# Decode attention beside an MLP on one core: `wo` is loaded and multiplied ahead of the first 16 rows of `w4`, and those rows go as four segments of 256 columns

## The chip, the core and the metric

The kernel runs on one core of one Trainium2 chip. The metric is the device time of one execution in microseconds (us); a kernel's time is the median of its runs. The engines are named as the profile names them: PE (TensorE matmuls), PEld (its weight loads), DVE (VectorE), ACT (ScalarE), POOL (GpSimd) and SP (SyncE, which here issues the transfers). A DMA transfer is served by 16 DMA engines.

## The reference, cut to what matters

```python
x  = A_x                                  # one token, 1024 numbers
xn = layernorm(x)
# branch A: one new token against a cache of 65536 positions, 32 query heads on 4 kv heads
q = (xn @ wq)                             # 1024 -> 4096
o = softmax(q @ k.T * 128**-0.5) @ v      # per head
A = o.reshape(1, 4096) @ wo               # 4096 -> 1024
# branch B
h  = gelu(layernorm(xn) @ w1); hs = shift(h) @ w2
x1 = xn + hs
B  = x1 + gelu(layernorm(x1) @ w3) @ w4   # 1024 -> 3584 -> 1024
out = x + A + B
```

All inputs are bf16. For a single token the shift leaves nothing of `h`, so `hs` is zero; the kernel still reads `w2`.

## The kernel before, in words

The cache of K and V is streamed once through SBUF. The loop runs over 32 subtiles of 8192 positions (`n` from 0 to 31), eight for each kv head. For each subtile DVE transposes K (`Ttr`, L493), PE multiplies it with the queries (`QK`, L503) into `S_ps`, a running softmax follows on DVE and ACT, PE multiplies with V (`PV`, L549) into `OT_ps`, and ACT and POOL add to the accumulator (`FLASH`). `KV` is one large SBUF tensor with two K slots (`KOFF`) and two V slots (`VOFF`), which later also hold the weight matrices.

All large transfers are issued by SP, one after the other, in the order in which the Python code calls `load_rows` (L319), `issue_k` and `issue_v`. Ahead of each, SP waits until the slot's readers are done; everything behind it on SP waits with it. At `n == 29`, `w1`, `w2` and `w3` are queued. At `n == 31` two more follow: the first 16 of the 28 row blocks of `w4` ("w40", 4096 KB) into K slot 1, which was last read by `QK(31)`; and `wo` (8192 KB) into V slot 1, which was last read by `PV(31)`. The other two parts of `w4` (`w4_parts`, L651: 10 blocks "w41", 2560 KB; 2 blocks "w42", 512 KB) go into K slot 0, once `w1` and `w2` there have been multiplied.

After the loop comes the epilogue on PE, in the order written: `w1`, `w2`, the small matmuls of a layer norm, the merging of the attention output into `o_bf` (L673 to L682), then `w3` (L464, 64 matmuls of 448 columns), whose gelu gives `gh_bf`. The last part is the two output projections. `gh_bf` has 28 columns of 128 numbers (one for each row block of `w4`) and `o_bf` has 32 (one for each row block of `wo`). A row block is a 128x1024 piece of a weight matrix; it is multiplied by its column in one of two helpers:

- `half_rows` (L663, matmul at L665): two matmuls of 512 columns on column tiles 0 and 32, summed in `S_ps`. Those sums are later copied to SBUF by DVE (`halves`, L692) and added into `OUT_ps` by four f32 matmuls with ones (L694, eight records in the profile).
- `out_rows` (L448, matmul at L452): four matmuls of 256 columns on the four column tiles, summed directly in `OUT_ps`.

Before, the first 16 blocks of `w4` and then all of `wo` go through `half_rows`; blocks 16 to 25 of `w4`, the L694 addition and the last two blocks go to `OUT_ps`. DVE then casts `OUT_ps` (L699) and SP sends the output (L700).

Of the kernel before, what the change touches and what calls it, by code (L numbers as in the profile page):

```python
# [144 lines left out]
def _grp(q, fns, reads=(), writes=(), partial=False):  # L145
    _deps(q, reads, writes)
    ev = None
    for i, fn in enumerate(fns):
        ev = q.op(fn, i == len(fns) - 1)
    _done(ev, reads, writes, partial)  # L150
    return ev
# [16 lines left out]
def bass_parallel_sum__gqa_block_cached__mixer_s_mlp__decode_kernel(  # L168
# [32 lines left out]
    with ExitStack() as es:  # L201
# [56 lines left out]
        KOFF, VOFF = (0, 16384), (32768, 65536)  # L258
# [41 lines left out]
        b_V = [_B(), _B()]  # L300
# [15 lines left out]
        def load_rows(dst, bufs, ch, w, r0, nrow):  # L316
            src = w.rearrange("(p r) n -> p (r n)", p=P)
            ncol = w.shape[1]
            _dma(q_sp, chan(ch), lambda e: e.dma_start(out=dst, in_=src[:, r0 * ncol:(r0 + nrow) * ncol]), writes=bufs)  # L319
# [128 lines left out]
        def out_rows(items, reads, last=False):  # L448
            fns = []
            for lhs, rhs in items:  # L450
                for jj in range(4):
                    fns.append(lambda e, lhs=lhs, rhs=rhs, jj=jj: e.matmul(  # L452
                        OUT_ps[32 * jj:32 * jj + 1, 0:256], lhs, rhs[:, 256 * jj:256 * jj + 256],
                        start=False, stop=last, tile_position=(0, 32 * jj), skip_group_check=True))
            _grp(q_pe, fns, reads=reads, writes=[b_OUT], partial=True)
# [28 lines left out]
        def Ttr(n, idx):  # L484
            if n >= NT:
                for ix in idx:
                    q_dve.op(lambda e, ix=ix: e.memset(spare[:, ix:ix + 1], 0.0))
                return
            s, half = (n // 2) % 2, n % 2
            for ix in idx:  # L490
                c = KOFF[s] // 2 + 4096 * half + 1024 * ix
                _deps(q_dve, [b_K[s][half]], [])
                ev = q_dve.op(lambda e, c=c: e.transpose(out=KV32[:, c:c + 1024], in_=KV32[:, c:c + 1024]))  # L493
                b_T[s][half].add_write(ev)

        def QK(n):
            s, half = (n // 2) % 2, n % 2
            fns = []
            for we in range(4):
                w_hi, e_ = divmod(we, 2)  # L500
                for cm in range(4):
                    mv = bass.AP(KV[:].tensor, KOFF[s] + half * 8192 + cm * 128 + w_hi * 64 + e_, [[kstep, P], [512, 16], [2, 32]])
                    fns.append(lambda e, we=we, cm=cm, mv=mv: e.matmul(  # L503
                        S_ps[32 * cm:32 * cm + 32, :], Ycur[:, we, :, :].rearrange("p a g -> p (a g)"), mv,
                        start=(we == 0), stop=(we == 3), tile_position=(0, 32 * cm)))
            _grp(q_pe, fns, reads=[b_T[s][half], b_Yc], writes=[b_S])

        def stats1(n):
            m = n % 2
            _op(q_dve, lambda e: e.reduce_max(mrow[:, m:m + 1], S_ps[:, :], axis=AX.X), reads=[b_S], writes=[b_mrow[m]])  # L510
            _op(q_dve, lambda e: e.tensor_tensor(out=Rm[:, m, :], in0=sel16[:, :], in1=mrow[:, m:m + 1].broadcast_to([P, 16]), op=ALU.mult),  # L511
                reads=[b_mrow[m], b_const], writes=[b_R[m]])

        def MB(n):
            m = n % 2
            _op(q_pe, lambda e: e.matmul(MB_ps[:, 0:16], Lmat[:, :], Rm[:, m, :], start=True, stop=True),  # L516
                reads=[b_R[m], b_const], writes=[b_MB])

        def stats2(n):
            _op(q_dve, lambda e: e.tensor_reduce(out=Bst[:, n % 4:n % 4 + 1], in_=MB_ps[:, 0:16], axis=AX.X, op=ALU.min),  # L520
                reads=[b_MB], writes=[b_Bcol[n % 4]])

        def EXP(n):
            m = n % 2
            ko = 1 - m
            cL = 513 * m
            if n % 4 == 0:
                q_dve.wait((s_b, n // 4 + 1))
            _op(q_dve, lambda e: e.tensor_tensor(out=brun[:, m:m + 1], in0=brun[:, ko:ko + 1], in1=Bst[:, n % 4:n % 4 + 1], op=ALU.min),  # L529
                reads=[b_brun[ko], b_Bcol[n % 4]], writes=[b_brun[m]])  # L530
            _op(q_act, lambda e: e.activation(p_sb[:, m, :], S_ps[:, :], ACTF.Exp, bias=brun[:, m:m + 1], scale=SCALE, accum_out=tmpO[:, cL:cL + 1]),  # L531
                reads=[b_S, b_brun[m]], writes=[b_p[m], b_tmpL[m]])
            _op(q_dve, lambda e: e.tensor_tensor(out=dd[:, m:m + 1], in0=brun[:, m:m + 1], in1=brun[:, ko:ko + 1], op=ALU.subtract),
                reads=[b_brun[ko], b_brun[m]], writes=[b_dd[m]])
            _op(q_act, lambda e: e.activation(ff[:, m:m + 1], dd[:, m:m + 1], ACTF.Exp), reads=[b_dd[m]], writes=[b_ff[m]])  # L535
# [43 lines left out]
        def load_at(c0, bufs, ch, w, r0, nrow):  # L579
            load_rows(KV[:, c0:c0 + nrow * w.shape[1]], bufs, ch, w, r0, nrow)  # L580
# [3 lines left out]
        for n in range(NT):  # L584
            if n % NSUB == 0:
                q_pe.mark(const_sems)
                q_pool.mark()
            if n % 4 == 0:
                q_act.mark()
            if n % 4 == 2:  # L590
                q_dve.mark(const_sems)
            if n == 0 or n % 4 == 2:
                Ttr(n, range(4))
            ahead = n + 1 if n % 4 != 1 else None
            if n % 4 != 1:
                QK(n)
            if ahead:
                Ttr(ahead, [0])
            stats1(n)
            MB(n)  # L600
            stats2(n)
            EXP(n)
            if ahead:
                Ttr(ahead, [1])
            PTr(n)
            if ahead:
                Ttr(ahead, [2, 3])
            if n % NSUB == NSUB - 1:
                head_switch(n // NSUB + 1)
            if n % 4 == 0:  # L610
                QK(n + 1)
            PV(n)
            FLASH(n)
            if n % NSUB == NSUB - 1:
                head_end(n // NSUB)
            if n % 2:
                issue_k((n + 3) // 2)
            if n % 4 == 1:
                issue_v((n + 3) // 4)
            if n == NT - 3:  # L620
                load_at(KOFF[0], b_K[0][:1] + b_T[0], "w1", B_w1, 0, 8)
                load_at(KOFF[0] + 8192, b_K[0][1:], "w2", B_w2, 0, 8)
                b_epi.r.update(b_V[0].r)
                load_at(VOFF[0], [b_V[0]], "w3", B_w3, 0, 8)
            if n == NT - 1:
                load_at(KOFF[1], b_K[1] + b_T[1], "w40", B_w4, 0, 16)
                load_at(VOFF[1], [b_V[1]], "wo", A_wo, 0, 32)
        for q in (q_pe, q_pool, q_act):
            q.mark(const_sems)

# [28 lines left out]
        def w4_rows(i):  # L659
            r0, nr, c0, b_w = w4_parts[i]  # L660
            return [(gh_bf[:, r:r + 1], KV[:, c0 + (r - r0) * D:c0 + (r - r0 + 1) * D]) for r in range(r0, r0 + nr)], [b_w, b_gh]

        def half_rows(items, reads):  # L663

            _grp(q_pe, [lambda e, lhs=lhs, rhs=rhs, jj=jj: e.matmul(  # L665
                S_ps[32 * jj:32 * jj + 1, :], lhs, rhs[:, 512 * jj:512 * jj + 512],
                start=False, stop=True, tile_position=(0, 32 * jj), skip_group_check=True)
                for lhs, rhs in items for jj in range(2)], reads=reads, writes=[b_S], partial=True)
# [17 lines left out]
        _op(q_dve, lambda e: e.transpose(out=ghT, in_=MM_ps[:, :].rearrange("p (b c) -> p b c", b=2)[:, :, 0:448].rearrange("p b (i r) -> p r b i", r=28)),  # L686
            reads=[b_M0, b_M1], writes=b_ge)
        gelu(tmp_flat[:, 0:896:32], KT_F, gh_bf[:, :], b_ge, [b_gh], (ge_x, ge_a, ge_b), b_ge)
        half_rows(*w4_rows(0))
        half_rows([(o_bf[:, r:r + 1], wo_sb[:, r * D:(r + 1) * D]) for r in range(32)], [b_V[1], b_o])  # L690
        halves = tmp_flat[0:64, 0:512]
        _op(q_dve, lambda e: e.tensor_copy(halves, S_ps[0:64, :]), reads=[b_S], writes=b_ge)  # L692
        out_rows(*w4_rows(1))
        _grp(q_pe, [lambda e, jj=jj: e.matmul(OUT_ps[32 * jj:32 * jj + 1, 0:256], ones_f[32 * (jj // 2):32 * (jj // 2) + 1, 0:1],  # L694
                                              tmp_flat[32 * (jj // 2):32 * (jj // 2) + 1, 256 * (jj % 2):256 * (jj % 2) + 256],
                                              start=False, stop=False, tile_position=(32 * (jj // 2), 32 * jj), skip_group_check=True)
                    for jj in range(4)], reads=b_ge + [b_const], writes=[b_OUT], partial=True)
        out_rows(*w4_rows(2), last=True)
        _op(q_dve, lambda e: e.tensor_copy(orow, OUT_ps[:, 0:256]), reads=[b_OUT], writes=[b_p[0]])  # L699
        ev_out = _dma(q_sp, chan("out"), lambda e: e.dma_start(out=out[0, 0, :].rearrange("(j n) -> j n", j=4), in_=orow[0:97:32, :]), reads=[b_p[0]])  # L700
# [35 lines left out]
```

## Time and profile before

| | |
|---|---|
| median of 3 runs | 405.1 us (404.21 to 405.42) |
| profiled execution | 405.76 us, of which the profile's span is 404.5 us |
| busy share of the span | PE 43%, DVE 58%, ACT 12%, POOL 23% |
| read from HBM | 169.87 MB, 420 GB/s over the span |
| last matmul group (L452) / cast of the output (L699) / issue of the output (L700) starts | 401.94 / 402.39 / 402.84 us |

Times in the profile's views count from the start of the span. The chain of waits is the sequence of work that ended last, followed back from the last instruction. A transfer's "us to landing" counts from the start of its issue on SP to the arrival of its last semaphore update. PEclk is the share of full clock that TensorE was granted; in this profile it is 0.50 or 1.00 at any one moment.

### The profile page before, as it was taken

The numbers are of one execution on the slowest core, as the hardware profiler recorded it, in microseconds if no ns is written. First come the engines' busy times: TensorE is split into PE (matmuls) and PEld (weight loads), VectorE is DVE, ScalarE is ACT, GpSimd is POOL, SyncE is SP. The second block draws the span as 40 slices with busy tenths as digits, with TensorE's granted clock in tenths as the row PEclk, the third lists the DMA queues.
The fourth block names the chain that finished last, engine by engine and source line by source line (L and its number), as shares of the span: only waits on it lengthen the run. The fifth ranks groups of instructions, "written<-read, shape, count | busy, mean of one in ns | idle before, by whom it ended". The sixth has DMA issues, their size and how long they took to land.

```text
span 404.5 us, 4599 instructions
## 1 busy us (share of the span) xinstructions
PE 172.8 (43%) x1472; PEld 53.3 (13%) x1472; DVE 233.4 (58%) x399; ACT 48.6 (12%) x132; POOL 91.3 (23%) x173
## 2 busy tenths in 40 slices
PE   0044242545253526434641544354424452546337
PEld 0022010111010101101110111011101110123113
DVE  0024756783787288648765875677567837554201
ACT  1000010211011101110201112012102110110000
POOL 6000021222035312230343121224312221340000
PEclk9998565566565555565566565556655565665959
DMA  9989999999999999999999999999999999999991
GB/s 382 447 373 457 416 425 486 424 388 441 431 442 421 424 457 428 412 434 476 428 402 428 434 467 395 424 470 415 418 467 437 395 424 438 454 417 459 421 391 58
DMA packets 4768, 169.98 MB, mean 420 GB/s; under 512 B 660, under 2 KB 664, under 8 KB 792
## 3 DMA queue, kind: packets, MB, share of 16 engines
q1 hardware_dynamic: 4616, 169.87, 97.5%
q8 instruction: 5, 0.08, 0.1%
q10 hardware_dynamic: 144, 0.00, 0.0%
q14 instruction: 3, 0.02, 0.0%
HBM read 169.87 MB, written 0.00 MB: 420 GB/s over the span
## 4 chain that ended last, share of the span: by engine, by line
DMA 56%; DVE 18%; PE 15%; issue 9%; ACT 1%; another core or an unknown queue 1%; DVEq 0%; POOL 0%; ACTq 0%; SPq 0%; POOLq 0%
DMA KV<-in_A_k_cache_dram 41%; DVE KV L493 13%; DMA KV<-in_A_wo_dram 9%; PE S_ps L503 8%; DMA x_bf<-in_A_x_dram 5%; PE S_ps L665 2%; DVE mrow L510 2%; PE PT_ps L539 2%; PE OT_ps L549 1%; ACT p_sb L531 1%; DVE pT_f L541 1%; PE MB_ps L516 1%; DVE Rm L511 0%; DVE Bst L520 0%
## 5 line engine op out<-in xcount | busy, mean ns | idle before, releaser
L493 DVE STREAM_TRANSPOSE KV<-KV 128x1024 f32<-128x1024 f32 x128 | 149.5, 1212 | 25.0 <-DMA KV<-in_A_k_cache_dram 25.0
L503 PE MATMUL S_ps<-KV,Ycur 128*32 128x512 bf16 x512 | 59.6, 613 | 87.0 <-DVE KV L493 86.7
L562 POOL TENSOR_TENSOR O_acc<-O_acc,tmpO 128x513 f32<-128x513 f32 x32 | 40.8, 1275 | 119.7 <-ACT tmpO L557 119.7
L549 PE MATMUL OT_ps<-KV,pT_f 128*32 128x512 bf16 x512 | 56.6, 590 | 19.5 <-DVE pT_f L541 18.6
L510 DVE TENSOR_REDUCE mrow<-S_ps 128x1 f32<-128x512 f32 x32 | 22.1, 692 | 39.0 <-PE S_ps L503 39.0
L531 ACT ACTIVATE p_sb<-S_ps,brun 128x512 bf16<-128x512 f32 x32 | 21.9, 686 | 139.6 <-DVE brun L529 122.7
L539 PE MATMUL PT_ps<-p_sb,permR 128*128 128x512 bf16 x32 | 17.0, 533 | 45.2 <-ACT p_sb L531 45.2
L557 ACT ACTIVATE tmpO<-OT_ps 128x512 f32<-128x512 f32 x32 | 19.2, 599 | 136.4 <-PE OT_ps L549 77.8
L503 PEld LDWEIGHTS S_ps<-KV,Ycur 128*32 128x32 bf16 x512 | 14.5, 126 | 127.3 <-DVE KV L493 98.3
L541 DVE STREAM_TRANSPOSE pT_f<-PT_ps 128x512 f32<-128x512 f32 x32 | 22.9, 714 | 12.4 <-PE PT_ps L539 11.5
L559 POOL TENSOR_TENSOR spare<-ff 128x1 f32<-128x1 f32 x32 | 6.2, 193 | 105.4 <-ACT ff L535 103.5
L560 POOL TENSOR_SCALAR O_acc<-O_acc,ff 128x514 f32<-128x514 f32 x32 | 22.4, 701 | 0.2 <-issue 0.2
L549 PEld LDWEIGHTS OT_ps<-KV,pT_f 128*32 128x32 bf16 x512 | 15.5, 128 | 49.4 <-DVE pT_f L541 28.6
L516 PE MATMUL MB_ps<-Rm,Lmat 128*128 128x16 bf16 x32 | 6.1, 192 | 25.5 <-DVE Rm L511 25.5
L692 DVE COPY KV<-S_ps 64x512 f32<-64x512 f32 x1 | 0.7, 682 | 23.2 <-PE S_ps L665 23.2
L665 PE MATMUL S_ps<-KV,o_bf 128*1 128x512 bf16 x64 | 10.0, 486 | 9.4 <-DMA KV<-in_A_wo_dram 9.4
L520 DVE TENSOR_REDUCE Bst<-MB_ps 128x1 f32<-128x16 f32 x32 | 5.6, 175 | 13.7 <-PE MB_ps L516 13.7
L381 PE MATMUL MM_ps<-ln_s,ones_f 128*128 128x1 f32 x6 | 1.8, 362 | 27.2 <-DVE ln_s L380 27.2
L377 DVE CAST xT<-x_bf 128x8 f32<-128x8 bf16 x1 | 0.2, 172 | 21.5 <-DMA x_bf<-in_A_x_dram 21.5
L516 PEld LDWEIGHTS MB_ps<-Rm,Lmat 128*128 128x128 bf16 x32 | 3.3, 102 | 52.3 <-DVE Rm L511 52.3
L393 POOL TENSOR_TENSOR ln_s<-ln_s,neghalf 128x1 f32<-128x1 f32 x3 | 1.7, 558 | 36.4 <-DVE ln_s L391 36.4
L539 PEld LDWEIGHTS PT_ps<-p_sb,permR 128*128 128x128 bf16 x32 | 3.2, 101 | 48.0 <-ACT p_sb L531 48.0
(114 smaller groups left out, 120.7 us busy)
## 6 DMA issues: line engine op xcount, KB each, us to landing
KV<-in_A_k_cache_dram SPq DMA_DIRECT2D x16, 4096.0 KB, 23.7
KV<-in_B_w_dram SPq DMA_DIRECT2D x1, 7168.0 KB, 33.2
KV<-in_B_w_dram SPq DMA_DIRECT2D x2, 2048.0 KB, 14.5
KV<-in_B_w_dram SPq DMA_DIRECT2D x1, 4096.0 KB, 22.0
KV<-in_B_w_dram SPq DMA_DIRECT2D x1, 2560.0 KB, 39.7
KV<-in_B_w_dram SPq DMA_DIRECT2D x1, 512.0 KB, 40.6
KV<-in_A_v_cache_dram SPq DMA_DIRECT2D x8, 36.1
x_bf<-in_A_x_dram ACTq DMA_DIRECT2D x1, 2.0 KB, 22.2
```

The costliest lines, as they stand in the source:

```text
L493: ev = q_dve.op(lambda e, c=c: e.transpose(out=KV32[:, c:c + 1024], in_=KV32[:, c:c + 1024]))
L503: fns.append(lambda e, we=we, cm=cm, mv=mv: e.matmul(S_ps[32 * cm:32 * cm + 32, :], Ycur[:, we, :, :].rearrange("p a g -> p (a g)"), mv, s ...
L510: _op(q_dve, lambda e: e.reduce_max(mrow[:, m:m + 1], S_ps[:, :], axis=AX.X), reads=[b_S], writes=[b_mrow[m]])
L516: _op(q_pe, lambda e: e.matmul(MB_ps[:, 0:16], Lmat[:, :], Rm[:, m, :], start=True, stop=True), reads=[b_R[m], b_const], writes=[b_MB])
L531: _op(q_act, lambda e: e.activation(p_sb[:, m, :], S_ps[:, :], ACTF.Exp, bias=brun[:, m:m + 1], scale=SCALE, accum_out=tmpO[:, cL:cL + 1]) ...
L539: _op(q_pe, lambda e: e.matmul(PT_ps[:, :], permR[:, :], p_sb[:, m, :], start=True, stop=True), reads=[b_p[m], b_const], writes=[b_PT])
L541: _op(q_dve, lambda e: e.transpose(out=pT_f[:, :], in_=PT_ps[:, :]), reads=[b_PT], writes=[b_pT])
L549: fns.append(lambda e, q=q, q4=q4: e.matmul(OT_ps[32 * q4:32 * q4 + 32, :], pT_bf[:, q, :, 1], KV[:, v0 + 512 * q:v0 + 512 * (q + 1)], sta ...
L557: _op(q_act, lambda e: e.activation(tmpO[:, 1:513], OT_ps[:, :], ACTF.Copy), reads=[b_OT], writes=[b_tmpO])
L560: b_Oacc.set_write(q_pool.op(lambda e: e.tensor_scalar(out=O_acc[:, :], in0=O_acc[:, :], scalar1=ff[:, m:m + 1], scalar2=0.0, op0=ALU.mult ...
L562: ev = q_pool.op(lambda e: e.tensor_tensor(out=O_acc[:, m:m + 513], in0=O_acc[:, m:m + 513], in1=tmpO[:, m:m + 513], op=ALU.add), tick=(s_ ...
L665: _grp(q_pe, [lambda e, lhs=lhs, rhs=rhs, jj=jj: e.matmul(S_ps[32 * jj:32 * jj + 1, :], lhs, rhs[:, 512 * jj:512 * jj + 512], start=False, ...
```

## The change

Two things change. At `n == 31` the load of `wo` is put ahead of the load of w40. In the epilogue, the first 16 row blocks of `w4` are no longer multiplied in `half_rows` ahead of `wo`, but in `out_rows` behind it; the L694 addition (L693 in the new file) now stands between them and blocks 16 to 25.

```diff
             if n == NT - 1:
+                load_at(VOFF[1], [b_V[1]], "wo", A_wo, 0, 32)
                 load_at(KOFF[1], b_K[1] + b_T[1], "w40", B_w4, 0, 16)
-                load_at(VOFF[1], [b_V[1]], "wo", A_wo, 0, 32)
...
         gelu(tmp_flat[:, 0:896:32], KT_F, gh_bf[:, :], b_ge, [b_gh], (ge_x, ge_a, ge_b), b_ge)
-        half_rows(*w4_rows(0))
         half_rows([(o_bf[:, r:r + 1], wo_sb[:, r * D:(r + 1) * D]) for r in range(32)], [b_V[1], b_o])
         halves = tmp_flat[0:64, 0:512]
         _op(q_dve, lambda e: e.tensor_copy(halves, S_ps[0:64, :]), reads=[b_S], writes=b_ge)
-        out_rows(*w4_rows(1))
+        out_rows(*w4_rows(0))
         _grp(q_pe, [lambda e, jj=jj: e.matmul(OUT_ps[32 * jj:32 * jj + 1, 0:256], ones_f[32 * (jj // 2):32 * (jj // 2) + 1, 0:1],
...
                     for jj in range(4)], reads=b_ge + [b_const], writes=[b_OUT], partial=True)
+        out_rows(*w4_rows(1))
         out_rows(*w4_rows(2), last=True)
```

In the order of PE's instructions, 32 matmuls of 512 columns in front of `wo`'s 64 are gone, and behind `wo` stand 64 matmuls of 256 columns (w40), the addition, and 48 of 256 columns (w41 and w42); before there were 40, the addition and 8. SP's two issues change places; DVE, ACT and POOL keep their order.

## The prediction

> **What bounds the kernel now.** I read first the page's slices for the DMA engines, since the kernel reads 169.87 MB once.
>
> ```profile
> DMA  9989999999999999999999999999999999999991
> GB/s 382 447 373 457 416 425 486 424 388 441 431 442 421 424 457 428 412 434 476 428 402 428 434 467 395 424 470 415 418 467 437 395 424 438 454 417 459 421 391 58
> ```
>
> A slice is 404.5 / 40 = 10.1 us. The transfers run without a pause until the last slice, where nearly nothing moves. So the time is the transfer stream plus what is left to do when it ends. The chain of waits, from 354 us on (start, duration, what), tells what that is:
>
> ```profile
> 354.63 35.76 DMA KV<-in_A_wo_dram
> 390.38 0.04 issue
> 390.43 9.43 PE S_ps L665 x59
> ...
> 400.28 1.20 PE OUT_ps L452 x35
> 401.48 0.54 PE OUT_ps L694 x8
> 402.01 0.35 PE OUT_ps L452 x8
> 402.36 0.02 issue
> 402.39 0.42 DVE p_sb L699
> ```
>
> PE waits for `wo` until 390.38, then works 12 us without a break. The DMA view, asked once for each of the last issues (KB, us from issue to landing), and SP's timeline with the issue times say where the rest of the stream ends:
>
> ```profile
> KV<-in_B_w_dram SPq DMA_DIRECT2D x1, 7168.0 KB, 33.2
> KV<-in_B_w_dram SPq DMA_DIRECT2D x1, 4096.0 KB, 22.0
> KV<-in_A_wo_dram SPq DMA_DIRECT2D x1, 35.8
> KV<-in_B_w_dram SPq DMA_DIRECT2D x1, 2560.0 KB, 39.7
> KV<-in_B_w_dram SPq DMA_DIRECT2D x1, 512.0 KB, 40.6
> ```
>
> ```profile
> 327.60 0.91 SPq L319 DMA_DIRECT2D KV<-in_B_w_dram  x2
> 349.06 0.33 SPq L319 DMA_DIRECT2D KV<-in_B_w_dram  x1
> 354.63 0.33 SPq L319 DMA_DIRECT2D KV<-in_A_wo_dram  x1
> 356.79 0.80 SPq L319 DMA_DIRECT2D KV<-in_B_w_dram  x2
> ```
>
> Issue plus landing time: `w3`, the second of the pair at 327.60 (so at about 328.1), lands at 361.3. w40, issued at 349.06, lands at 371.1. `wo` (354.63) lands at 390.4, w41 (356.79) at 396.5, w42 (about 357.2) at 397.8. The gaps are 9.8, 19.3, 6.1 and 1.3 us for 4.19, 8.39, 2.62 and 0.52 MB: about 430 GB/s each. The transfers are thus served in the order of issue, each at the full rate, and the stream ends at 397.8. But the cast L699 starts at 402.39. The 4.6 us between are PE's own backlog, since half of its work behind `wo` could not start until `wo` was there. The PE timeline shows the other side:
>
> ```profile
> 377.40 3.62 PE L665 MATMUL S_ps<-KV,gh_bf 128*1 128x512 bf16 x32 [2.89 <-DVE gh_bf L478]
> 390.43 9.53 PE L665 MATMUL S_ps<-KV,o_bf 128*1 128x512 bf16 x60 [9.41 <-DMA KV<-in_A_wo_dram]
> ```
>
> w40's matmuls take 3.62 us under cover, then PE stands idle for 9.41 us.
>
> **The change part by part.** *The issues.* SP now waits for `PV(31)` first and issues `wo` at 354.63 as before; w40 stands behind that wait and goes at about 355.0 instead of 349.06. Behind them, w41 and w42 wait for the `w2` matmuls anyway and keep 356.8. The moved wait costs nothing as long as the DMA engines have other work: `w3` feeds them until 361.3, 6.7 us past 354.63. A transfer into an idle stream needs a start: `wq`, the first, took 22.0 us for the size that took `wo` 19.3 within the stream, so 2.7 us. Cover left: 6.7 - 2.7 = 4.0 us. If the cover were gone, every us of idle stream would come back in full.
>
> *The landings.* The same bytes in another order: `wo` at 361.3 + 19.3 = 380.7 (9.7 earlier), w40 at 380.7 + 9.7 = 390.4 (19.3 later), w41 still at 396.5 and w42 at 397.8.
>
> *wo on PE.* `o_bf` is ready at 372.4 and `w3`'s matmuls end at 374.5, so the 64 matmuls start at 380.7. Before, from 390.43 to 400.28, they took 9.85 us, the first part at half clock. Half clock gives a pair of 512 columns 0.426 us (weight loads in the timeline at 390.81, 391.24, 391.66), full clock 32 matmuls in 3.4 us, 0.213 a pair. PE's idle before them is now 6.2 us (374.5 to 380.7), so I keep the cold start and the 9.85 us: they end at 390.5. All of it lies beside w40's transfer. Cold throughout would be 32 x 0.426 = 13.6 us, to 394.3; that is the upper end.
>
> *w40 on PE.* Removed: 32 matmuls, 3.62 us, all hidden, worth 0. Added: 64 of 256 columns at the end of `wo`, when w40 has just landed. The trace has 32 matmuls of this width on four tiles (L464 with `g_bf`): their weight loads go out in 0.87 us at full clock, 0.109 a row of four. The chain has 35 of L452 in 1.20 us, 0.137 a row. Half clock: rows of four of 448 columns go every 0.374 us (weight loads at 370.60, 370.98, 371.35), so 256 columns need 0.213. Hence 16 rows take 1.7 to 3.4 us. The clock should be full after 9 us of work, so 1.7, to 392.2. The copy (0.68) runs beside these rows, and the addition (0.54 to 0.61) ends by 392.9. w41 is there only at 396.5, so all this hides with 3.6 us to spare.
>
> *The new tail.* PE idles from about 392.9 to 396.5, and the clock in the tail is the open price. The windows view (busy times, then PEclk, DMA share, GB/s) shows the gate before:
>
> ```profile
> 351.94:355.35 3.41, 2.72 (x36) 1.45 (x40) 0.66 (x3) 0.60 (x1) 0.69 (x2) 0.50 1.09 471
> 355.36:358.76 3.40, 1.38 (x52) 1.03 (x40) 2.22 (x6) 0.42 (x1) 3.19 (x6) 1.00 0.86 373
> 379.26:382.66 3.40, 1.76 (x18) 0.53 (x12) 0.00 (x0) 0.00 (x0) 0.00 (x0) 1.00 0.89 386
> 386.09:389.49 3.40, 0.00 (x0) 0.00 (x0) 0.00 (x0) 0.00 (x0) 0.00 (x0) 0.50 0.63 272
> ```
>
> The clock changes on a grid of 3.41 us. A stretch with PE busy for 2.72 of 3.41 us is followed by full clock; one with 1.38 is followed by half (the stretch after 358.76 begins at 0.50); one with 1.76 stays. So a grid stretch that is mostly idle between 392.9 and 396.5 drops the clock, before w41 for some positions of the grid and during it for most others. Full clock: 10 rows x 0.109 = 1.1 us, 397.6; then w42, landed 397.8, with 0.39 for its two rows, to 398.2. Half clock: 10 x 0.213 = 2.1, 398.65; w42 is long there and takes 2 x 0.213 plus the drain (0.39 - 0.22 = 0.17), 0.6, to 399.25. With 0.06 to the cast, L699 starts at 398.3 or 399.3 instead of 402.39: a gain of 4.1 or 3.1 us. In the grid of this trace the drop would come at 396.3, and most positions give half clock for most of the rows, so I take 3.1. What follows L699 keeps its length, 404.5 - 402.39 = 2.1 us.
>
> The Trainium skill ("TensorE: Matmul & The Clock Gate", section "Why this matters for your kernels") speaks against the new order: it asks for no idle gap over about 3 us between bursts of matmuls, since one idle window brings the clock back to half. By the row that is nearest, the 5.1 us from 381.0 to 386.1 during which the idle PE kept its full clock, the gap of 3.6 us would leave w41 at full clock and the gain at 4.1; by the page's rule it is 3.1.
>
> *The sum.* Profiled span 404.5 - 3.1 = 401.4, execution 405.76 - 3.1 = 402.7. The profiled execution lies 0.66 above the median, so the median goes from 405.1 to 402.0.
>
> **The rivals.** *PE becomes the bound.* The clock stays at half from 380.7 on. `wo` ends at 394.3, w40's rows take 3.4 (397.7), the addition up to 1.0, w41 2.1 and w42 0.6: 401.4, gain 0.9, 404.2 us. For it: half clock holds in most slices. Against it: 5.9 us of work brought the clock back at 396.3.
>
> *The queued transfers share the engines.* This is the slower side. Before, w40 was issued 5.6 us ahead of `wo`; now the two follow within 0.4 us. If the engines served them together, `wo` would land with w40 at 390.4, and w40's rows would come on top of the old tail: 390.4 + 9.85 + 1.7 + 0.6 + 1.1 + 0.4 = 404.05 against 402.36, plus 1.7, 406.8 us. It decides once `wo` lands after 388.7. Against it: `w1`, `w2` and `w3`, issued within 1.3 us, land at about 339.4, 344.4 and 361.3, in order.
>
> *Nothing to win.* The stream stretches in the tail, or breaks off at 354.6 because PV(31) is late by more than the 4.0 us of cover. A break of 3.1 us gives 405.1. Against it: all views of this stretch show the engines full. That the loads don't change places can be left out: SP's instructions stand in the new order.
>
> **How the numbers follow.** Forecast with either clock in the tail: 0.87. PE as the bound: 0.05. Sharing: 0.04. Stream broken or stretched: 0.04. About 0.3%, 1.2 us, is what a measurement of this kernel can tell from no change, so faster means under 403.9. The forecast is faster; PE as the bound (404.2) counts as same by a hair, split 0.03 faster and 0.02 same; sharing is slower; the broken stream is 0.02 same, 0.01 each side. That is faster 0.91, same 0.04, slower 0.05. Range: the full clock gives 405.1 - 4.1 = 401.0, and the runs before spread 1.2 us, half of it below, 400.4. Above, the half clock's 402.0 plus half the spread is 402.6; the rest, to 403.4, reaches halfway from there to the PE-bound case at 404.2.
>
> **What would show it.** In the changed profile: `wo` issued near 354.6 and w40 right behind; the wait of PE for `wo` ends near 380.7; L665 with `o_bf` ends near 390; a PE idle of 3 to 4 us that w41 ends, near 396.5; L699 between 398.3 and 399.3; the chain running through w41's or w42's transfer instead of `wo`'s. It is wrong if `wo` lands after 388, if w42 lands later than 398.5, or if PE shows no idle time ahead of w41.

## The result, and the profile after

| | before | changed |
|---|---|---|
| median, first comparison (5 runs each) | 405.1 us (404.21 to 405.49) | 402.81 us (402.08 to 403.26) |
| ratio, 95% interval | | 0.9947 (0.9928 to 0.9966) |
| second comparison, another chip (23 and 5 runs) | 405.3 us (404.3 to 406.0) | 402.68 us (402.04 to 402.73) |
| ratio, 95% interval | | 0.9926 (0.9913 to 0.9939) |
| profiled execution, span | 405.76, 404.5 us | 402.08, 400.8 us |

The changed kernel is faster by 2.3 and 2.6 us in the medians and by 2.1 and 3.0 us by the ratios; 3.1 was forecast. The two profiled executions lie 3.7 us apart, which overstates it: the one before is slower than all five of its runs in the table, the changed one is the fastest of its five. The chain of waits of the changed kernel, its end:

```profile
357.65 39.11 DMA KV<-in_B_w_dram
...
396.80 1.88 PE OUT_ps L452 x47
...
398.70 0.42 DVE p_sb L699
```

The transfer in the chain is now w41, not `wo`, and only 1.9 us of PE's work stand behind it where there were 12. The DMA view of the last four issues, and SP's timeline with their starts:

```profile
KV<-in_A_wo_dram SPq DMA_DIRECT2D x1, 26.1
KV<-in_B_w_dram SPq DMA_DIRECT2D x1, 4096.0 KB, 35.4
KV<-in_B_w_dram SPq DMA_DIRECT2D x1, 2560.0 KB, 39.1
KV<-in_B_w_dram SPq DMA_DIRECT2D x1, 512.0 KB, 40.0
```

```profile
354.82 0.33 SPq L319 DMA_DIRECT2D KV<-in_A_wo_dram  x1
355.27 0.36 SPq L319 DMA_DIRECT2D KV<-in_B_w_dram  x1
357.65 0.81 SPq L319 DMA_DIRECT2D KV<-in_B_w_dram  x2
```

`wo` lands at 380.9, w40 at 390.7, w41 at 396.8 and w42, issued at about 358.0, at 398.0. The stream ends where it ended (397.8 before); what stood behind it is gone. PE's timeline of the tail:

```profile
380.99 8.64 PE L665 MATMUL S_ps<-KV,o_bf 128*1 128x512 bf16 x64 [5.56 <-DMA KV<-in_A_wo_dram]
390.70 1.92 PE L452 MATMUL OUT_ps<-KV,gh_bf 128*1 128x256 bf16 x64 [1.07 <-DMA KV<-in_B_w_dram]
...
396.80 1.84 PE L452 MATMUL OUT_ps<-KV,gh_bf 128*1 128x256 bf16 x48 [3.64 <-DMA KV<-in_B_w_dram]
```

In this execution each burst ends before the next transfer lands: PE waits 1.07 us for w40 and 3.64 us for w41. The windows view of a second profile of the changed kernel (e11 below; busy times, PEclk, DMA share, GB/s) shows what that last wait does to the clock:

```profile
393.15:396.56 3.41, 0.00 (x1) 0.00 (x1) 0.00 (x0) 0.00 (x0) 0.00 (x0) 1.00 0.75 304
396.58:399.98 3.40, 2.71 (x48) 1.41 (x48) 0.43 (x1) 0.00 (x0) 0.00 (x0) 0.50 0.04 16
```

There a whole grid stretch lay inside the wait, w41's and w42's 48 matmuls ran at half clock and took 2.73 us, and L699 started at 399.34. In the first profile the clock held until 397.86, for most of the rows, and L699 started at 398.70.

### The profile page after: what moved, and what is told of

Its sections match the earlier page's. It is cut to its first block, busy times and chain, and to the rows that moved or that the text cites. A ratio compares the mean times of both kernels' runs of the same rounds, so it can differ in the third digit from the quotient of the medians.

```text
span 400.8 us, 4663 instructions
## 1 busy us (share of the span) xinstructions
PE 175.5 (44%) x1504; PEld 54.0 (13%) x1504; DVE 232.5 (58%) x399; ACT 48.6 (12%) x132; POOL 91.5 (23%) x173
## 4 chain that ended last, share of the span: by engine, by line
DMA 57%; DVE 18%; PE 13%; issue 10%; ACT 1%; another core or an unknown queue 0%; DVEq 0%; POOL 0%; ACTq 0%; SPq 0%; POOLq 0%
DMA KV<-in_A_k_cache_dram 42%; DVE KV L493 13%; DMA KV<-in_B_w_dram 10%; PE S_ps L503 9%; DMA x_bf<-in_A_x_dram 6%; DVE mrow L510 2%; PE PT_ps L539 2%; PE OT_ps L549 1%; PE MM_ps L464 1%; ACT p_sb L531 1%; DVE pT_f L541 1%; PE MB_ps L516 1%; PE OUT_ps L452 0%; DVE Rm L511 0%; DVE Bst L520 0%
## 5 line engine op out<-in xcount | busy, mean ns | idle before, releaser
L549 PE MATMUL OT_ps<-KV,pT_f 128*32 128x512 bf16 x512 | 58.7, 609 | 19.5 <-DVE pT_f L541 18.7
L665 PE MATMUL S_ps<-KV,o_bf 128*1 128x512 bf16 x64 | 8.6, 437 | 5.6 <-DMA KV<-in_A_wo_dram 5.6
```

The costliest lines, as they stand in the source:

```text
L549: fns.append(lambda e, q=q, q4=q4: e.matmul(OT_ps[32 * q4:32 * q4 + 32, :], pT_bf[:, q, :, 1], KV[:, v0 + 512 * q:v0 + 512 * (q + 1)], sta ...
L665: _grp(q_pe, [lambda e, lhs=lhs, rhs=rhs, jj=jj: e.matmul(S_ps[32 * jj:32 * jj + 1, :], lhs, rhs[:, 512 * jj:512 * jj + 512], start=False, ...
```

## The experiments

The theory: the end is the end of the stream plus what PE still has to do then, and the change moves `wo`'s burst under w40's transfer. Its rivals are that the four short segments bring the gain (form), or that PE's clock does. Comparisons ran on several chips, each beside the kernel before, whose median was 405.0 to 405.3 us.

**e1: the order alone.**

```diff
# against before; the two loads change places as in the change
-        half_rows(*w4_rows(0))
         half_rows([(o_bf[:, r:r + 1], wo_sb[:, r * D:(r + 1) * D]) for r in range(32)], [b_V[1], b_o])
+        half_rows(*w4_rows(0))
```

> New order of loads and of matmuls (wo first, then w40), but w40's 16 row blocks keep two segments of 512 columns in S_ps; the copy and the addition stand where they stood before, ahead of the last two row blocks. Backlog theory (the stream of loads ends at about 398 and the change moves PE's work under it): most of the gain stays. w40's rows run from about 390.7 for 3.4 us, still hidden, and only the addition (0.55 us) comes back between w41 and w42, so the cast starts 0.4 to 0.6 us later than in the changed kernel; median 1.3 to 2.5 us below before. Form theory (the four short segments bring the gain, because they need half of PE's time): no gain, about 405.1 us. Clock theory (the gain is that PE is granted full clock earlier): as the changed kernel, 402.8 us.

Measured: 402.32 us, ratio 0.9946 (0.9925 to 0.9966), as large a gain as the change's. End of its chain:

```profile
396.57 1.26 PE OUT_ps L452 x40
397.83 0.54 PE OUT_ps L694 x8
...
398.74 0.42 DVE p_sb L699
```

The addition came back onto the path, but in this execution the rows ran at full clock, so L699 starts where it does in the first profile of the changed kernel. The form theory falls. The 0.4 to 0.6 us expected against the changed kernel cannot be told apart from the clock's spread.

**e2: the form alone.**

```diff
# against before
-        half_rows(*w4_rows(0))
+        out_rows(*w4_rows(0))
         half_rows([(o_bf[:, r:r + 1], wo_sb[:, r * D:(r + 1) * D]) for r in range(32)], [b_V[1], b_o])
```

> Old order of loads and of matmuls, but w40's 16 row blocks go in four segments of 256 columns into OUT_ps. Backlog theory: these rows lie in PE's wait for wo, so 1.8 us less of them is worth 0: 405.1 us, within 0.3%. Form theory: 1.8 us or more is gained. Clock theory: 0 too.

Measured: 404.67 us, ratio 0.9994 (0.9983 to 1.0005), no difference. w40's rows took 1.92 us instead of 3.62, inside PE's wait for `wo`, worth nothing.

**e3 and e4: half of the reordering each.** e3 is the changed kernel with the two loads back in the old order; e4 is the kernel before with the two loads in the new order.

> The changed kernel's order on PE (wo, then w40 in four segments, the addition, w41, w42) with the old order of loads (w40 first). Backlog theory: wo still lands at 390.4 and w40's rows now stand behind it, uncovered: 16 x 0.109 = 1.7 us slower than before, 406.8 us, with the chain through wo's load. Form theory: faster than before by about 2 us. Clock theory: about as before.

> The changed kernel's order of loads (wo first) with the old order on PE (w40 in two segments first, then wo). Backlog theory: PE stands waiting for w40 until 390.5 though wo landed at 381, then has 48 row blocks in two segments to do: 3.4 us slower than before, 408.5 us, with the chain through w40's load. Form theory: as before. Clock theory: as before, since PE's idle time ahead of the burst is 13 us.

Measured: e3 407.14 us (ratio 1.0047, 1.0031 to 1.0062), e4 408.32 us (1.0081, 1.0062 to 1.0101). The ends of the two chains, e3 first:

```profile
390.43 9.33 PE S_ps L665 x59
...
400.20 1.85 PE OUT_ps L452 x59
...
404.05 0.42 DVE p_sb L699
```

```profile
390.35 11.84 PE S_ps L665 x91
...
404.72 0.42 DVE p_sb L699
```

In e3 w40's rows stand uncovered behind `wo`, in e4 both matrices wait for w40. Each half alone is a loss of the size that the backlog gives; only together do they gain.

**e5: PE kept busy in the last wait.** The changed kernel with this ahead of w41's rows:

```diff
+        _grp(q_pe, [lambda e: e.matmul(PT_ps[:, :], permR[:, :], KV[:, VOFF[1]:VOFF[1] + 512], start=True, stop=True)
+                    for _ in range(13)], reads=[b_V[1], b_const], writes=[b_PT])
         out_rows(*w4_rows(1))
```

> The changed kernel with 13 more matmuls of 512 columns (into an unused PSUM bank, nobody reads them) between the addition and w41's rows, to keep PE busy for 2.8 of the 3.7 us in which it waits for w41. Backlog theory with the clock term of the prediction: the work is hidden, w41's and w42's rows always run at full clock, the cast starts 0.4 to 0.6 us after w42's landing; against the changed kernel's median a gain of 0 to 1 us, about 0.5: 402.3 us. If the tail's clock has no part in the median: 402.8 us, same as the changed kernel.

Measured: 401.74 us (401.58 to 402.17), ratio to before 0.9923 (0.9910 to 0.9936), 1.1 us below the changed kernel's first median. w41's and w42's rows took 1.63 us, and the cast (L701 there) started at 398.35, the prediction's full-clock value. The end of its chain:

```profile
396.67 1.66 PE OUT_ps L452 x48
398.33 0.02 issue
398.35 0.42 DVE p_sb L701
```

So the clock in the tail costs the changed kernel some 0.7 to 1.0 us in the median. The two kernels were not run on one chip; each against the kernel before on its own chip, the medians differ by 3.3 us in e5 and by 2.3 and 2.6 in the changed kernel, and e5's interval overlaps that of the second comparison. The size is firmer in single executions: the cast starts 0.5 us behind w42's landing in e5 and 1.6 us behind it in e11.

**e6 and e12: PE kept busy in the old wait.** The kernel before with extra matmuls between w40's rows and `wo`'s, 38 in e6 and 26 in e12:

```diff
# against before
         half_rows(*w4_rows(0))
+        _grp(q_pe, [lambda e: e.matmul(PT_ps[:, :], permR[:, :], KV[:, KOFF[1]:KOFF[1] + 512], start=True, stop=True)
+                    for _ in range(38)], reads=[b_K[1][0], b_const], writes=[b_PT])
```

> The kernel before with 38 more matmuls of 512 columns (into an unused PSUM bank) behind w40's rows, so that PE is busy for 8.1 of the 9.4 us in which it waits for wo. Backlog theory: wo's 32 row blocks then run at full clock from 390.4, 6.8 us instead of 9.85, and the tail ends about 399.3 instead of 402.4: 2.3 to 3 us below before, but with the cast still 1.5 us behind w42's landing, so not faster than the changed kernel, and the chain still through wo's load. Clock theory (the clock at the start of the burst is the whole of the gain): the same time as the changed kernel and nothing left to gain from the order. If the cold start had no part in the time: 405.1 us.

> The kernel before with 26 instead of 38 extra matmuls of 512 columns in PE's wait for wo, so that they are done before wo lands whatever the clock. Backlog theory: wo's burst at full clock takes 6.8 us from 390.6, the cast starts at about 399.5, 1.6 us behind w42's landing; 402.7 us, 0.9 us slower than the changed kernel with its warm gap (401.7). Clock theory (the cold start is the whole of what the change removes): 401.7 us, the same as that one.

Measured: e6 403.0 us (402.88 to 404.5), ratio 0.9958 (0.9943 to 0.9972). In its profile, the slowest of its six runs, w40's rows began at half clock and took 5.04 us, so the extra matmuls started late and ran 1.5 us past `wo`'s landing (392.06 instead of 390.6). e12 went the other way: 404.66 us, ratio 0.9974 (0.9957 to 0.9991), with single runs from 402.81 to 405.99. In its profile the extra matmuls were done at 386.7, and the wait of 4.08 us that was left was enough for the clock to fall again (windows view; the second line begins 1.2 us ahead of `wo`'s burst):

```profile
386.13:389.53 3.40, 0.54 (x3) 0.05 (x1) 0.00 (x0) 0.00 (x0) 0.00 (x0) 1.00 0.66 284
389.55:392.95 3.40, 2.20 (x12) 0.74 (x14) 0.00 (x0) 0.00 (x0) 0.00 (x0) 0.50 0.99 422
```

As designed both missed. e6's median cannot be told apart from the changed kernel's 402.8 us, but the changed kernel's tail is partly or wholly cold in both of its profiles; the fair partner is e5, whose tail is at full clock. The fastest runs of e6 and e12, 402.88 and 402.81 us, stand 1.2 to 1.3 us above e5's fastest, 401.58. e6's profile gives the same, for there `wo`'s burst ran at full clock from its start:

```profile
392.13 6.47 PE S_ps L665 x59
...
401.13 0.42 DVE p_sb L701
```

From the burst's start at 392.06 to the cast are 9.07 us. Started when `wo` landed (390.56), it would have ended at 399.6, 1.75 us behind w42's landing (397.88) where e5 ends 0.48 behind it: an estimate of 1.3 us for the order alone, at full clock in both. So the clock is not the whole of the gain, but it is about half of it: 5.9 us of `wo`'s burst at half clock cost the old tail 2.9 us, while a cold new tail costs 1.1. e12's runs spread by 3.2 us, and its one profiled execution, of 405.95 us, had the burst at half clock for 5.6 us, worth 2.8.

**e7: the wait on SP made longer.** The changed kernel with the two loads called behind L644, ahead of them a wait for its transpose.

```diff
-            if n == NT - 1:
-                load_at(VOFF[1], [b_V[1]], "wo", A_wo, 0, 32)
-                load_at(KOFF[1], b_K[1] + b_T[1], "w40", B_w4, 0, 16)
...
+        for b in (b_p[1],):
+            for s_, v_ in b.w.items():
+                q_sp.wait((s_, v_))
+        load_at(VOFF[1], [b_V[1]], "wo", A_wo, 0, 32)
+        load_at(KOFF[1], b_K[1] + b_T[1], "w40", B_w4, 0, 16)
```

> The changed kernel, but wo, w40, w41 and w42 are issued only after the transpose at L644, at about 361.5 instead of 354.8, just as w3's transfer ends. Term under test: the cover of SP's wait, put at 4.0 us (w3 feeds the engines until 361.1, and a transfer into an idle stream needs a start of 2.7 us). With that start: the stream breaks for about 3 us, wo lands at about 383.7, all later landings and the end move by 2.8 us: 405.6 us. Without a start time: 403.2 us.

Measured: 406.96 us, 4.2 above the changed kernel's 402.81. The DMA view of `wo`'s issue, which started at 361.90, and the windows view of the same stretch in e7 and in the changed kernel:

```profile
KV<-in_A_wo_dram SPq DMA_DIRECT2D x1, 22.9
```

```profile
359.00:362.50 3.50, 0.57 (x8) 0.10 (x8) 2.63 (x8) 0.00 (x0) 2.10 (x6) 0.90 0.00 0
```

```profile
359.00:362.50 3.50, 0.88 (x8) 0.10 (x8) 2.36 (x7) 0.00 (x0) 1.79 (x5) 0.69 0.87 374
```

The view counts a packet in the stretch in which it begins. In e7 none begins between 359.0 and 362.5, and w42 lands 3.9 us later (401.9 instead of 398.0). A `wo` that finds the stream drained lands 22.9 us after its issue; fed, it landed 19.9 us after `w3` in the changed kernel (361.0 to 380.9) and 19.5 us after it in e1 (361.2 to 380.7). The start is thus 3.0 to 3.4 us, not 2.7, and the change's wait had 361.0 - 354.8 = 6.2 us less that, 2.8 to 3.2 us of cover, not 4.0. The expectation of 405.6 us was 1.4 short: the landings moved by 1.1 us more than it said, and the tail was cold (48 matmuls in 2.73 us). The Trainium skill ("DMA: Bandwidth & Descriptors", section "Anatomy of one DMA — SWDGE (gpsimd) path") gives, for transfers issued by GpSimd, 2.0 us plus bytes at 436 GB/s, from which one would estimate 21.2 us for `wo`; no run here issues it from GpSimd, and for this one from SP the measured 22.9 decide.

**e9: w2 is not read.** The changed kernel without the load of `w2`.

> The changed kernel without the load of w2 (2.1 MB); the matmuls at w2's place stay and multiply what lies in the slot by the zeros that stand for hs's input, so only the reading of w2 is left out. Backlog theory: the end hangs on the stream's end, so 2.10 MB at 430 GB/s, 4.9 us, come off in full: 397.9 us. If PE's work behind the landings is the bound: less than 3 us.

Measured: 400.18 us, ratio 0.9885 (0.9871 to 0.9899): 2.6 us below the changed kernel instead of 4.9. The stream broke: `w3` now lands at 356.1, only 1.3 us behind `wo`'s issue at 354.82, and `wo` takes 23.0 us to land as in e7; fed, it would have landed at 356.1 + 19.9 = 376.0 instead of 377.8. That returns 1.8 us of the 4.9. The other 0.6 is in the tail: the cast starts 1.3 us behind w42's landing (394.9) instead of 0.7, with the last 48 matmuls partly at half clock, 2.32 us against 1.84.

**e13: the gap refilled.** As e9, but blocks 16 to 23 of `w4` take `w2`'s place in the queue, the last 4 blocks come last, and PE multiplies the 8 ahead of `wo`. The zeros multiply `w1`'s slot, so that only the reading of `w2` is left out.

```diff
# against the changed kernel
-                load_at(KOFF[0] + 8192, b_K[0][1:], "w2", B_w2, 0, 8)
+                load_at(KOFF[0] + 8192, b_K[0][1:], "w2", B_w4, 16, 8)
...
-        quad_rows(M1_ps, [b_M1], (g_bf, b_const), KV[:, 8192:16384], b_K[0][1], 256)
+        quad_rows(M1_ps, [b_M1], (g_bf, b_const), KV[:, 0:8192], b_K[0][0], 256)
...
-        w4_parts = [(0, 16, KOFF[1], b_K[1][0]), (16, 10, KOFF[0], _B()), (26, 2, KOFF[0] + 10 * D, _B())]
+        w4_parts = [(0, 16, KOFF[1], b_K[1][0]), (16, 8, KOFF[0] + 8192, b_K[0][1]), (24, 4, KOFF[0], _B())]
...
-            if i:
+            if i == 2:
...
+        out_rows(*w4_rows(1))
         half_rows([(o_bf[:, r:r + 1], wo_sb[:, r * D:(r + 1) * D]) for r in range(32)], [b_V[1], b_o])
...
-        out_rows(*w4_rows(1))
         out_rows(*w4_rows(2), last=True)
```

> The changed kernel without reading w2 (the zeros that stand for hs's input multiply w1's slot instead), but with 8 row blocks of w4 loaded at w2's place in the queue and in SBUF, and the last 4 row blocks as the last load; PE multiplies the 8 ahead of wo. If the missing 2.3 us of the run without w2 went into a break of the stream at wo's issue (cover too short): w3 ends at about 356.1, the 8 row blocks at 361.0, no break, the last load lands at 393.1, 4.9 us earlier, and the cast starts 0.6 to 1.2 us later: 397.4 to 398.0 us. If it went into PE's tail: 400 us again.

Measured: 397.03 us (396.9 to 397.13), ratio 0.9793 (0.9781 to 0.9806), the fastest run, and below the expected range. The end of its chain:

```profile
390.52 1.92 PE OUT_ps L452 x64
...
392.98 0.64 PE OUT_ps L452 x16
...
393.64 0.42 DVE p_sb L699
```

The 8 blocks stand ahead of `w3` in the queue, not behind it as the expectation had it; `w3` lands at 361.2 as with `w2`, and so the stream does not break. The last load lands at 392.9, 5.1 us earlier than in the changed kernel, and PE goes through the tail almost without a wait, at full clock. e13 changes two things at once: the stream is 2.1 MB shorter, and of the work behind w40 only 16 matmuls are left where there were 48. The addition ends at 392.98, just as the last load lands, so stream and PE end together here. For the kernel's own task, which has `w2` read, e5 is the fastest version that was run.

**e10 and e11: both kernels once more.**

> The kernel before once more, for a second profile of it. Clock-phase theory of the size (the sum was made against one execution whose wo burst happened to run 5.9 us at half clock, near the long end; the typical cold start is shorter): wo lands at 390.4 to 390.7 as before, the cold part of the burst is shorter than 5.9 us, and the cast starts half as much earlier, at 401.2 to 401.9 instead of 402.4; the median stays at 405. Rival (the profiled execution was typical, and the 3.7 us between the two profiled executions is the true gain): cold part 5.9 us again, cast at 402.4.

> The changed kernel once more, for a second profile and its time on this chip. Backlog theory: w42 lands at 397.7 to 398.0, the cast starts 0.5 us (all rows at full clock) to 1.6 us (all at half clock) later; 402.8 us in the median, 402.0 to 403.6 in single runs. If the first profile's tail (0.7 us) were typical: 402.1 us in the median.

Measured: e10 405.39 us (404.37 to 405.62); its profiled execution, 405.62, again had `wo`'s burst at half clock for 5.9 us, and L699 at 402.25. The expectation of a shorter cold part missed: this is the rival's number. But this execution, too, was the slowest of its ten. e11 gave 402.68 us, with the cold tail shown above.

## Why the prediction was right, point by point

- *The stream sets the end, and 4.6 us of PE's backlog stood behind it.* Right; the landings came within 0.3 us of those worked out, and L699 follows w42's landing by 0.7 and 1.6 us in the two profiles. e13 fits the stream as the bound: its last load lands 5.1 us earlier, and its median is 4.7 us below that of e5, whose tail is at full clock too (another chip). e9 fits it once the break of the stream is counted.
- *The moved wait costs nothing.* Right, with a cover of 2.8 to 3.2 us where the step said 4.0, since the start is 3.0 to 3.4 us (e7). w41 was issued at 357.65 and not at 356.8, as the matmuls with `w1` and `w2` ran longer at half clock in this execution; with `wo` and w40 queued ahead of it that cost nothing.
- *The new segments are worth 0.* Right (e2: 0.9994; e1 gains without them).
- *`wo`'s burst hides beside w40.* Right: 8.64 us in the first profile and 9.81 in the second, done at 389.6 and 390.5. In the second that is 0.1 us after w40's landing, so nothing was to spare there.
- *The clock in the tail, L699 at 398.3 or 399.3.* The cold end was seen, 399.34, and once a value between the two, 398.70; the other end was seen only with PE kept busy, 398.35 (e5). Of the two readings that the prediction set side by side, the rule of about 3 us was the safer one: after the waits of 3.65 and 3.64 us the clock fell at 396.54, as w41 landed, in the second profile and at 397.86, 1.1 us into the rows, in the first.
- *The rivals.* `wo` landed 9.7 us ahead of w40, so the transfers don't share. PE was not the bound, since it waited for w41 by 3.6 us in both profiles. A stretch or break of the stream occurred only where it was made (e7, e9).
- *The size, 3.1 in place of 2.3 and 2.6.* The second comparison's interval, 2.5 to 3.5 us of 405.3, holds it; the first's, 1.4 to 2.9 us of 405.1, doesn't quite. By the ratios, 2.1 and 3.0 us, the miss lies in the first comparison alone. The likely term is the last one of the sum: the 0.66 us by which the profiled execution lay above the median were carried over to the changed kernel as if they were common to both. In e2, whose tail is that of before, `wo`'s burst was cold for 3.7 us instead of 5.9 and L699 started at 401.52, 0.9 us earlier, though `wo` landed 0.2 us later. So part of the old tail was the long cold stretch of that one execution, and without the 0.66 the sum gives 402.7, which is what the profiled execution with the cold tail took (e11, 402.73). That the faster runs of the kernel before have the shorter cold stretch is argued from e2 and e12 and not shown: both its own profiles had the long one.

## What to carry to other kernels

Where a stream of loads fills the time, compare the last landing with the last instruction: the difference is compute that arrives too late, and the operand with the most work behind it should land first, with loads and matmuls reordered together, since either alone loses. Before a wait is moved on the issuing engine, count how long the transfers already queued will run past it, less the start of a transfer into an idle stream. A sum made against one execution should say which of its terms, here the clock's phase, differ between executions before an offset to the median is carried over.

## What the runs showed of the hardware that was not expected

- The kernel with the 26 extra matmuls (e12) ran in 402.8 to 406.0 us, in three groups of four near 403.0, 404.6 and 405.8. Its one profiled execution, of the slowest group, had the clock fall 1.2 us ahead of the last long burst. That the groups differ by where the clock's grid falls in the wait of about 4 us is argued from this one profile and not shown, since no faster execution was profiled.
- PE's busy time in a grid stretch doesn't settle what the clock does next. It fell after stretches with 0.00, 0.54 and (before) 1.38 us of 3.4, but near 1.5 us both were seen. It held after 1.46 (the first profile of the changed kernel) and fell after 1.64 (e4, in the loop):

```profile
373.97:377.38 3.41, 1.46 (x32) 0.58 (x24) 1.75 (x5) 0.00 (x0) 0.00 (x0) 1.00 0.81 346
377.39:380.79 3.40, 0.00 (x0) 0.00 (x0) 0.46 (x3) 0.23 (x1) 0.00 (x0) 1.00 0.96 414
```

```profile
32.31:35.72 3.41, 1.64 (x32) 0.74 (x24) 1.46 (x5) 0.60 (x1) 0.00 (x0) 1.00 0.71 308
35.73:39.13 3.40, 0.29 (x2) 0.29 (x2) 2.63 (x15) 0.00 (x0) 0.00 (x0) 0.50 1.16 501
```

- The way up is as unsharp. It rose after 2.71 us (e11, 396.58 to 399.98) and did not rise after 2.20 (e12) and 2.47 (before, 389.50 to 392.90), nor after 2.85 in e6:

```profile
368.05:371.45 3.40, 2.85 (x14) 0.92 (x18) 1.20 (x3) 0.00 (x0) 0.00 (x0) 0.50 1.34 578
371.47:374.87 3.40, 3.40 (x44) 1.43 (x40) 1.19 (x2) 0.00 (x0) 0.00 (x0) 0.50 0.79 332
```

The ends of matmuls are modelled in the profile, so these busy times carry an error of their own.
